# A first chunk's exponentials four heads at a time, finer gate steps, and a new order of the front

## The chip, the cores and the metric

The kernel runs on one core of a Trainium2 chip. The metric is device time in microseconds (us) of one execution. The kernel before takes 463.09 us, the median of three runs (462.23, 463.09 and 463.59).

The core has five engines, each with its own instruction queue that is worked off in order: TensorE (PE in the profile; its weight loads are shown as PEld), VectorE (DVE), ScalarE (ACT), GpSimd (POOL) and SyncE (SP). SP here issues nearly all transfers. Engines wait for each other by semaphores. TensorE writes its results into PSUM, a small memory of banks.

## The reference

An mLSTM cell over 4 batches, 8 heads, 768 time steps and 40 values per head, with a gate on its output, and behind it a two-layer network with an exact GELU. All is float32.

```python
for t in range(S):
    m_new = np.maximum(f_gate[:, :, t] + m, i_gate[:, :, t])
    f_stab = np.exp(f_gate[:, :, t] + m - m_new)
    i_stab = np.exp(i_gate[:, :, t] - m_new)
    m = m_new
    C = f_stab * C + i_stab * einsum('bhd,bhe->bhde', vt, kt)
    n = f_stab * n + i_stab * kt
    denom = np.maximum(np.abs(nq), 1.0)          # nq = n . q
    y[:, :, t] = sigmoid(o_gate[:, :, t]) * (C q) / denom
x = y as (3072 tokens, 320)
out = gelu(x @ w_in) @ w_out                     # w_in 320x2048, w_out 2048x320
```

The network's weights come as 64-bit floats, which the kernel reads as pairs of 32-bit words and turns into float32 itself.

## The kernel before

**Tiling.** The 768 steps are six chunks of 128. Within a chunk the cell is worked out like masked attention: scores of k and q, times a weight W = exp(a[key] - M[query]) where the key isn't behind the query, and then times v. What earlier chunks left is a state per batch and head. a, M and the decays come from the gates: bl is the running sum of f within a chunk, a = i - bl, M the running maximum of a, m0 the maximum carried from chunk to chunk. These gate tiles have 32 partitions (batch and head) and one row of 128 per chunk.

**Stages.** The program has a front and then five rounds. The front works out the gates, chunks 0 and 1 of the cell, and the network for chunk 0. Each later round works out one chunk of the cell beside the network for the chunk before. This case is about the front.

**The order.** In each engine's queue instructions stand in the order in which the program emits them. For the front that order is written out by hand in a string, `FRONT`. Each word is a step: a letter and, where needed, numbers (a batch, a chunk, a count). `play` runs them one after another, and each step puts its instructions into the queues of all engines that it uses. The letters:

- chunk 0 in lower case, chunk 1 in upper case, the number is the batch: `w`/`W` weights (the exponentials W, on ACT), `M` mask (POOL), `g`/`G` sigmoid of the output gate (ACT), `t`/`T` k and q transposed by TensorE and copied by ACT, `s`/`S` scores on TensorE and their product with W on VectorE, `c`/`C` the state carried on, `v`/`V` values on TensorE, `y`/`Y` finish (VectorE), `x`/`X` y transposed for the network, `R` split of x.
- `L` loads q and k, `O` loads v and the output gate, `B` loads M of chunk 1 for one batch (the number runs over batches of all chunks, so `L4` is batch 0 of chunk 1).
- `P` fetches a piece of the network's weights, `K` converts the next fetched piece on ACT (two activations), `J` ends that on VectorE (two instructions) and fetches the piece four further on. There are four buffers for fetched pieces, ten pieces of w_in and sixteen of w_out.
- `A` and `U` are the network's up steps for the first and the second half of chunk 0's tokens, four each, with a GELU on ACT behind each; two that follow each other directly are run as a pair. `F` is one of sixteen rows of the down product. `Z` splits a weight for the next round.
- `E` the gates of chunk 1, `N` those of chunks 2 to 5 with their decays, `D`, `Q`, `d`, `q` the decays transposed and spread, `r` and `p` send some of these out and back, `e` first blocks of chunk 2, `H` frees the gate tiles.
- `k` n: n matmuls whose result nobody reads. `I` n: n such matmuls ahead of the next step that writes a fresh bank. Both keep TensorE going.

**The exponentials of chunk 0.** In `Cell.weights`, for chunk 0, M has to be spread over all 128 partitions. It is cut into three bf16 parts (`M_parts`, 96 partitions), and for each head one matmul with a row of an identity (`row`) puts M of that head into a bank `pm` that holds four heads (L460). A matmul with `beyond`, 1e30 where the key is behind the query, adds the mask (L462). The exponential is then taken head by head, since a is added as the activation's bias, one value per partition: eight activations of 128x128 for each batch (L465). aT is a turned by TensorE (`gates_turned`, L252 and L253). Chunk 1 has M from a transfer (`load_M`) and uses the same L465.

**Lines that the steps touch.** Fillers L226 (`warm`) and L398 (`unread`); gates L270 to L277; M_parts L308 and L310; conversion L374, L375 (ACT), L385, L386 (VectorE), fetch L364; scores L537 and L540; state L575 to L595; values L655; finish L672 to L677; y transposed L695, its copy into first_x L700; up steps L804, L810 and GELU L814; down rows L1042; the next round's products L947.

Of the kernel before, what the change touches and what calls it, by code (L numbers as in the profile page):

```python
# [9 lines left out]
F32 = mybir.dt.float32  # L10
F32R = mybir.dt.float32r
BF16 = mybir.dt.bfloat16
U32 = mybir.dt.uint32
AF = mybir.ActivationFunctionType
OP = mybir.AluOpType

P = 128
# [7 lines left out]


FRONT = """
    I2 O0 g0 L0 P0 L1 E k1 t0 P1 P2 w0 k7 N k2 w1 O1 K L2 Q s0 O3 w2 q D
    k2 d P3 t1 w3 c0 L3 J v0 t2 K K y0 s1 I7 v1 I8 O2 J g1 L4 I5 c1 K I1
    I2 y1 s2 x0 t3 B4 O4 B5 g2 J x1 s3 v2 c2 L5 y2 H T0 x2 G0 v3 g3 c3 K y3  # L30
    M1 J L6 J A x3 M0 K W0 O7 K A O6 O5 J M2 W1 S0 C0 K J J T1 U U
    K L7 V0 K T2 r J J A G2 K G1 Y0 W2 S1 K M3 C1 A J S2 J K W3 K
    V1 C2 Y1 T3 J J U U S3 V2 K K J G3 J Y2 C3 X0 K V3 J K F J F
    K K B8 F J K F F J K F F F R0 X1 J J K F J F K X2 F J
    K F J Y3 K F R1 e J F Z B9 B10 F X3 R2 Z R3 F p"""
DOWN = """
    M0 F Z F L3 W0 M1 Z W1 S0 C0 F F h0 Q2 F K2 G1 D3 B3 Z V0 G2 M2 W2 M3 W3 V1 K3 Q3 F G0 S2 Z Y0 G3 C2 h2 F
    F Y1 X0 V2 V3 F N F j R0 Y2 Y3 X1 F F X2 R1 F R2 X3 R3 F"""
# [3 lines left out]
def kernel(  # L42
# [16 lines left out]
    nc = tc.nc  # L59

    B, H, S, D = q.shape
    L = P
    NCH = S // L
# [3 lines left out]
    BH = B * H  # L67
# [45 lines left out]
    W = {n: shared([P, H, L], F32, f"W{n}") for n in range(B - 1)}  # L113
# [7 lines left out]
    eye = gates.tile([P, P], BF16, name="eye")  # L121
    beyond = gates.tile([P, L], BF16, name="beyond")
# [15 lines left out]
    def swapped(c, b):  # L138

        return c > 1 and b % 2 == 1  # L140

    def load(n, first=0, end=4):

        if n >= NCH * B:
            return
        c, b = divmod(n, B)
        for src, dst in ((q, qb), (k, kb), (v, vb), (o_gate, None))[first:end]:
            if dst and swapped(c, b):
                x, to = src[b, :, c * L:(c + 1) * L, :].rearrange("h p d -> p h d"), dst[turn_of(n)][:, :, 0:D]
# [24 lines left out]
    def turn_of(n):  # L174

        return n % NLD if n < 2 * B else (n - 2 * B) % NQ
# [31 lines left out]

    keep = gates.tile([BH, NCH, L], F32, name="keep")
    bl = gates.tile([BH, NCH, L], F32, name="bl")  # L210
    a = gates.tile([BH, NCH, L], F32, name="a")
    M = gates.tile([BH, NCH, L], F32, name="M")
    ew = gates.tile([BH, NCH - 1, L], F32, name="ew")
    gg = gates.tile([BH, NCH - 1, L], F32, name="gg")
    m0 = gates.tile([BH, NCH], F32, name="m0")
    M_left = gg[:, 0:2]
    M_parts = gates.tile([3 * BH, L], BF16, name="M_parts")
    row = gates.tile([3 * BH, BH], BF16, name="row")
    for j in range(3):
        m = slice(BH * j, BH * (j + 1))  # L220
        nc.scalar.copy(out=row[m], in_=ident[m, m])

    def warm(n):
        cold = ps_h.tile([P, P], F32, name="cold", tag="h")
# [21 lines left out]
    def gates_turned(*parts):  # L246

        for src, dst in parts:
            n = dst.shape[1]
            pg = ps_tr.tile([P, n, BH], F32, name="pg", tag="tr")  # L250
            for c in range(n):
                nc.tensor.transpose(pg[:, c, :], src[:, c, :], ident[0:BH, 0:BH])  # L252
            nc.vector.tensor_copy(out=dst, in_=pg)  # L253
# [12 lines left out]

    def gates_of(c0, c1):

        flat = lambda t: t[:, c0:c1].rearrange("p c l -> p (c l)")
        nc.vector.tensor_tensor_scan(out=flat(bl), data0=flat(keep), data1=flat(f_sb), initial=0.0,  # L270
                                     op0=OP.mult, op1=OP.add)
        nc.vector.tensor_tensor(out=a[:, c0:c1], in0=i_sb[:, c0:c1], in1=bl[:, c0:c1], op=OP.subtract)
        for c in range(c0, c1):
            nc.vector.tensor_tensor_scan(out=M[:, c], data0=a[:, c], data1=a[:, c], initial=m0[:, c:c + 1],
                                         op0=OP.max, op1=OP.max)
            if c + 1 < NCH:
                nc.vector.tensor_tensor(out=m0[:, c + 1:c + 2], in0=bl[:, c, L - 1:L], in1=M[:, c, L - 1:L],  # L277
                                        op=OP.add)

    def decays_of(e0, e1, g0, g1):  # L280

        e, g = slice(e0, e1), slice(g0, g1)
        nc.vector.tensor_tensor(out=ew[:, e], in0=a[:, e], in1=M[:, e, L - 1:L].to_broadcast([BH, e1 - e0, L]),
                                op=OP.subtract)
        nc.vector.tensor_tensor(out=gg[:, g], in0=m0[:, g0 + 1:g1 + 1].unsqueeze(2).to_broadcast([BH, g1 - g0, L]),
                                in1=M[:, g0 + 1:g1 + 1], op=OP.subtract)
        nc.scalar.activation(out=ew[:, e], in_=ew[:, e], func=AF.Exp)
        nc.scalar.activation(out=gg[:, g], in_=gg[:, g], func=AF.Exp)
# [13 lines left out]


    gates_of(0, 1)
    left = M[:, 0]
    for j in range(3):
        part = M_parts[BH * j:BH * (j + 1)]
        nc.vector.tensor_copy(out=part, in_=left)  # L308
        if j < 2:
            nc.vector.tensor_tensor(out=M_left[:, j], in0=left, in1=part, op=OP.subtract)  # L310
            left = M_left[:, j]
    gates_turned((a[:, 0:1], aT[:, 0:1]))
    warm(6)

    def second_gates():
        gates_of(1, 2)
        nc.sync.dma_start(out=M_d[0], in_=M[:, 1])
        gates_turned((a[:, 1:2], aT[:, 1:2]))
        decays_of(0, 2, 0, 1)

    def later_gates():
        gates_of(2, NCH)
        nc.sync.dma_start(out=M_d[1:].rearrange("c p l -> p c l"), in_=M[:, 2:])
        gates_turned((a[:, 2:], aT[:, 2:]))
        decays_of(2, NCH - 1, 1, NCH - 1)


    w_src = {}
# [67 lines left out]
    def unread(bank):  # L396
        for _ in range(idle[0]):
            nc.tensor.matmul(bank, ident, ident, start=True, stop=True, skip_group_check=True)  # L398
        idle[0] = 0
# [25 lines left out]
    class Cell:  # L425
# [16 lines left out]
        def weights(self, b):  # L442

            n = self.c * B + b
            if self.c > 0:
                W[n] = M_n = Mb.pop(n)
            elif n not in W:
                W[n] = wts.tile([P, H, L], F32, name="W", tag="W")
            for h in range(H):
                r = b * H + h  # L450
                if self.c > 0:
                    src = M_n[:, h, :]
                else:


                    if h % 4 == 0:
                        pm = ps_mm.tile([P, 4, L], F32, name="pm", tag="b")
                        unread(pm[:, 0, :])
                        for j in range(4):
                            nc.tensor.matmul(pm[:, j, :], row[:, r + j:r + j + 1].to_broadcast([3 * BH, P]), M_parts,  # L460
                                             start=(j == 0), stop=False, skip_group_check=True)
                        nc.tensor.matmul(pm, eye, beyond.unsqueeze(1).to_broadcast([P, 4, L]), start=False, stop=True,  # L462
                                         skip_group_check=True)
                    src = pm[:, h % 4, :]
                nc.scalar.activation(out=W[n][:, h, :], in_=src, func=AF.Exp, scale=-1.0, bias=aT[:, self.c, r:r + 1])  # L465
            if n in (B, B + 1):
                load_M(n + 2)
# [666 lines left out]
    def first_blocks():  # L1134

        copy_chunk(2, range(1))
        for r in (32, 96):
# [2 lines left out]

    first_g = Hidden(False)
    n_pieces = range(len(pieces))
    steps = dict(P=fetch, L=lambda n: load(n, 0, 2), O=lambda n: load(n, 2, 4), B=load_M, E=second_gates, N=later_gates,
                 I=keep_clock, k=warm, D=lambda: decays_turned(0, 2, 0, 1), Q=lambda: decays_turned(2, NCH - 1, 1, NCH - 1),
                 d=lambda: decays_last(0, 1), q=lambda: decays_last(1, NCH - 1), r=halves_out, p=halves_back,
                 A=in_turn(first_up_steps(0)), U=in_turn(first_up_steps(1)), e=first_blocks, F=in_turn(first_down_steps(first_g)),
                 K=in_turn(lambda i=i: conv_one(i) for i in n_pieces), H=products_begin,
                 J=in_turn(lambda i=i: conv_two(i) for i in n_pieces), Z=split_weight)
    steps |= cell_steps(0, "mwgtscvyx") | cell_steps(1, "MWGTSCVYXR")
    play(FRONT, steps)  # L1150
    for c in range(1, NCH):
# [6 lines left out]
        steps = cell_steps(c + 1, "MWGTscVYXRLKQDCBSjh", g)  # L1158
# [36 lines left out]
```

## Time and profile before

| | |
|---|---|
| median of three runs | 463.09 us |
| the profiled execution | 462.86 us |
| its span, first to last instruction | 460.7 us |
| TensorE busy | 451.9 us, 98% |
| VectorE busy | 308.7 us, 67% |
| ACT busy | 243.7 us, 53% |
| GpSimd busy | 76.7 us, 17% |
| granted TensorE clock | 1.000 |
| TensorE's share of the chain that ended last | 95% |
| first up step, first down row, end of the front | 40.2, 91.7 and 127.3 us |

The profile is of one execution. Busy time is summed over the instructions of an engine, and idle time is put down to what ended it. The chain of work that ended last is followed back from the last instruction, at each step to what released it. A down row, an up step or a transposition in float32 shows as one or two records for each matmul of the program.

### The profile page before, as it was taken

How to read it: one execution, taken by the hardware profiler on the slowest of the kernel's cores; microseconds unless marked ns; L12 is line 12 of the kernel's file. 1: busy time of each engine (PE TensorE's matmuls, PEld its weight loads, DVE VectorE, ACT ScalarE, POOL GpSimd, SP SyncE). 2: the span in 40 equal slices, each digit the busy share in tenths (PEclk: the TensorE clock that was granted, in tenths of full speed). 3: DMA queues.
4: the chain of work that ended last, by engine and by line, in shares of the span. 5: the costliest groups of instructions: out<-in, count | busy, mean ns of one | idle time of the engine just before them, and what ended most of it. 6: DMA issues, size and time to landing. Idle time of an engine off the chain costs nothing.

```text
span 460.7 us, 13113 instructions
## 1 busy us (share of the span) xinstructions
PE 451.9 (98%) x5432; PEld 402.0 (87%) x5432; DVE 308.7 (67%) x661; ACT 243.7 (53%) x541; POOL 76.7 (17%) x117
## 2 busy tenths in 40 slices
PE   9999999999999998999999999999999999999996
PEld 8787888877788898998899998899998899988996
DVE  8677457573579987755578754578654577699950
ACT  7886999953244593113494113395113395257701
POOL 3001030000010432200542200542300422100000
PEclk9999999999999999999999999999999999999999
DMA  7999962295857655219945219853018950200001
GB/s 168 221 221 223 232 177 69 82 242 125 166 129 158 113 96 98 57 51 182 167 79 103 59 57 184 154 92 46 3 57 168 172 94 15 80 35 1 1 0 58
DMA packets 174875, 51.12 MB, mean 111 GB/s; under 512 B 154752, under 2 KB 168352, under 8 KB 174816
## 3 DMA queue, kind: packets, MB, share of 16 engines
q1 hardware_dynamic: 174496, 49.95, 51.0%
q8 instruction: 43, 0.70, 0.6%
q10 hardware_dynamic: 320, 0.33, 0.2%
q14 instruction: 16, 0.13, 0.1%
HBM read 45.47 MB, written 10.03 MB: 120 GB/s over the span
## 4 chain that ended last, share of the span: by engine, by line
PE 95%; DVE 2%; issue 1%; DMA 1%; ACT 1%; SPq 0%; DVEq 0%
PE po L1063 26%; PE pu L947 23%; PE po L1042 8%; PE pu L804 6%; PE pu L958 6%; PE po L917 6%; PE ph L655 4%; PE ps L553 3%; PE pu L810 2%; PE ps L537 2%; PE px L695 2%; PE pf L608 2%; PE pt L515 1%; PE cold L226 1%; PE pf L619 1%; PE pf L575 1%
## 5 line engine op out<-in xcount | busy, mean ns | idle before, releaser
L1063 PE MATMUL po<-w_out,g 128*128 128x160 f32 x512 | 74.4, 302 | 0.0
L962 ACT ACTIVATE g<-pu 128x512 f32<-128x512 f32 x64 | 32.2, 618 | 77.4 <-PE pu L958 77.4
L1063 PEld LDWEIGHTS po<-w_out,g 128*128 128x128 f32 x512 | 70.1, 190 | 1.9 <-ACT g L962 1.3
L947 PE MATMUL pu<-x_hi,w_in_hi 128*128 128x512 f32 x160 | 39.0, 387 | 0.0
L465 ACT ACTIVATE W<-W,aT 128x128 f32<-128x128 f32 x128 | 38.7, 387 | 0.1
L947 PE MATMUL pu<-x_lo,w_in_lo 128*128 128x512 f32 x160 | 37.8, 379 | 0.0
L1063 PE MATMUL po<-w_sums,sums 128*128 128x160 f32 x256 | 36.9, 302 | 0.0
L439 POOL TENSOR_SCALAR_AFFINE_SELECT W<-W 128x1024 f32<-128x1024 f32 (+2 forms) x20 | 24.1, 1209 | 75.8 <-DMA W<-M_d 66.8
L1063 PEld LDWEIGHTS po<-w_sums,sums 128*128 128x128 f32 x256 | 35.0, 190 | 0.4
L1042 PE MATMUL po<-w_out,g 128*128 128x320 f32 x128 | 35.2, 433 | 0.0
L947 PEld LDWEIGHTS pu<-x_hi,w_in_hi 128*128 128x128 f32 x160 | 29.5, 189 | 5.7 <-ACT g L962 1.3
L947 PEld LDWEIGHTS pu<-x_lo,w_in_lo 128*128 128x128 f32 x160 | 30.2, 189 | 4.3
L1042 PEld LDWEIGHTS po<-w_out,g 128*128 128x128 f32 x128 | 24.0, 190 | 9.6
L524 POOL TENSOR_TENSOR vw<-vb,ewT 128x328 f32<-128x328 f32 x12 | 8.7, 737 | 138.5 <-DMA vb<-in_v_dram 55.9
L947 PE MATMUL pu<-x_all,w_mid 128*128 128x512 f32 x80 | 30.3, 379 | 0.0
L947 PE MATMUL pu<-x_all,w_in_mid 128*128 128x512 f32 x80 | 30.3, 379 | 0.0
L559 DVE TENSOR_TENSOR W<-ps,W 128x256 f32<-128x256 f32 (+1 forms) x48 | 18.1, 416 | 17.0 <-PE ps L553 7.1
L804 PE MATMUL pu<-first_x,w_in 128*128 128x256 f32 x128 | 28.8, 381 | 0.0
L804 PEld LDWEIGHTS pu<-first_x,w_in 128*128 128x128 f32 x128 | 23.8, 190 | 3.1
L791 DVE TENSOR_TENSOR sums<-g 128x512 f32<-128x512 f32 x16 | 12.3, 770 | 19.6 <-ACT g L962 19.6
L763 DVE TENSOR_TENSOR w_in_mid<-w_in_hi,w_in_lo 128x512 fp32r<-128x512 f32 x20 | 13.7, 686 | 16.5 <-PE pu L947 16.5
L385 DVE SCALAR_TENSOR_TENSOR pow<-sig,pow 128x320 uint32<-128x320 uint32 (+1 forms) x26 | 14.6, 563 | 13.7 <-ACT pow L375 13.7
(195 smaller groups left out, 917.5 us busy)
## 6 DMA issues: line engine op xcount, KB each, us to landing
W<-M_d SPq DMA_DIRECT2D x16, 512.0 KB, 5.4
bits<-in_moe_w_in_dram SPq DMA_DIRECT2D x20, 256.0 KB, 4.5
bits<-in_moe_w_out_dram SPq DMA_DIRECT2D x16, 320.0 KB, 3.2
blocks<-kq_d SPq DMA_DIRECT2D x32, 128.0 KB, 3.6
ob<-in_o_gate_dram SPq DMA_DIRECT2D x24, 160.0 KB, 3.9
out_dram<-o_sb SPq DMA_DIRECT2D x36, 80.0 KB, 2.0
kq_d<-in_k_dram SPq DMA_DIRECT2D x32, 80.0 KB, 2.5
kq_d<-in_q_dram SPq DMA_DIRECT2D x32, 80.0 KB, 2.5
```

Of the source, the lines that this page charges most:

```text
L385: nc.vector.scalar_tensor_tensor(out=p, in0=s, scalar=3, in1=p, op0=OP.logical_shift_left, op1=OP.bitwise_or)
L439: nc.gpsimd.affine_select(out=x, in_=x, compare_op=OP.is_ge, fill=1.0e30, base=base, pattern=[[0, H], [1, x.shape[2]]], channel_multiplier=-1)
L465: nc.scalar.activation(out=W[n][:, h, :], in_=src, func=AF.Exp, scale=-1.0, bias=aT[:, self.c, r:r + 1])
L559: nc.vector.tensor_tensor(out=w[r, :, t], in0=ps[i][hip][r, :, t], in1=w[r, :, t], op=OP.mult)
L655: nc.tensor.matmul(ph[r, h, :], Pm[:, h, r], vb[turn_of(n)][:, h, :], start=True, stop=True)
L804: nc.tensor.matmul(banks[-1][e][:, i - i0, :], in_tile(i, x)[:, e, i % 2 * P:(i % 2 + 1) * P], first_x[:, x, t0:t1], start=(x == 0 and i = ...
L917: nc.tensor.matmul(in_pairs(po[t]), x[:, t * L:(t + 1) * L], in_turns(w), start=(f, k) == first, stop=(f, k) == last, skip_group_check=True)
L947: nc.tensor.matmul(in_pairs(pus[i][e]), w[k][:, e, i * P:(i + 1) * P], in_turns(x[:, k, :]), start=(n == 0 and k == 0), stop=False, skip_g ...
L958: nc.tensor.matmul(in_pairs(pu[e]), w[r, i // 2, i % 2 * P:(i % 2 + 1) * P], in_turns(x[r, NX, :]), start=False, stop=(n == 2), skip_group ...
L962: nc.scalar.activation(out=g.t[:, HF * e + i, :], in_=pu[e], func=AF.Gelu, scale=4097.0)
L1042: nc.tensor.matmul(po[b], g.t[:, f, b * L:(b + 1) * L], w_out[:, f, :], start=(f == 0), stop=(f == NF - 1))
L1063: nc.tensor.matmul(bank[k][:, t, :], lhs(j, t), rhs(j), start=(first and t == 0 and j == 0), stop=(t == 1 and j == HF - 1), skip_group_che ...
```

## The change

Three things are changed, all in the front.

1. **Chunk 0's exponentials.** a and M become two halves of one tile aM, and both are cut into three bf16 parts (`aM_parts`). `row` gets a second half with its sign turned. For each bank of four heads one matmul of 512 columns, with a's parts as the weights and the negated rows of four heads spread over 128 columns each, puts -a into the bank; four matmuls add M as before, and one the mask. One activation then takes the exponentials of four heads, 128x512, without a bias. aT of chunk 0 is no longer needed and its transposition goes.
2. **Later gates in parts.** `later_gates` (one step `N` for chunks 2 to 5) becomes `sums_of` for one chunk (`N2` to `N5`), `largest_of` for one chunk (`n2` to `n5`), the later decays (`l`), and the sending out and turning (`o`).
3. **The order.** All of `FRONT` is replaced. The old order has 28 fillers by `k` and `I`, the new one 19.

```diff
 FRONT = """
-    I2 O0 g0 L0 P0 L1 E k1 t0 P1 P2 w0 k7 N k2 w1 O1 K L2 Q s0 O3 w2 q D
-    k2 d P3 t1 w3 c0 L3 J v0 t2 K K y0 s1 I7 v1 I8 O2 J g1 L4 I5 c1 K I1
-    I2 y1 s2 x0 t3 B4 O4 B5 g2 J x1 s3 v2 c2 L5 y2 H T0 x2 G0 v3 g3 c3 K y3
-    M1 J L6 J A x3 M0 K W0 O7 K A O6 O5 J M2 W1 S0 C0 K J J T1 U U
-    K L7 V0 K T2 r J J A G2 K G1 Y0 W2 S1 K M3 C1 A J S2 J K W3 K
-    V1 C2 Y1 T3 J J U U S3 V2 K K J G3 J Y2 C3 X0 K V3 J K F J F
-    K K B8 F J K F F J K F F F R0 X1 J J K F J F K X2 F J
-    K F J Y3 K F R1 e J F Z B9 B10 F X3 R2 Z R3 F p"""
+    k2 L0 O0 t0 P0 N2 O1 N3 P1 L1 w0 k3 P2 N4 g0 E O3 n2 I5 w1 L2 N5 k7 n3 n4 n5 l Q t1 L3 K s0 K D J w2 q v0
+    w3 c0 y0 s1 g1 k2 K L4 O2 v1 t2 J P3 c1 y1 x0 g2 d s2 t3 O4 v2 c2 x1 B4 J y2 K s3 T0 g3 B5 x2 J K v3 A M1
+    y3 L5 K L6 M0 J x3 o J K W0 H K W1 A c3 O7 S0 C0 U J M2 O6 G0 O5 K K J J T1 r L7 e U A J T2 V0 K W2 S1 J K
+    S2 A G2 C1 G1 Y0 V1 U M3 J C2 K W3 V2 K T3 U J Z K Y1 J S3 K J K J J p K K C3 J G3 K F K F Y2 F K J F J V3
+    B8 X0 J B9 K K F R0 F X1 F K F X2 F F J J J F Y3 F R1 X3 B10 F R2 K F J F R3 J Z F"""
...
     for j in range(3):
         m = slice(BH * j, BH * (j + 1))
-        nc.scalar.copy(out=row[m], in_=ident[m, m])
+        nc.scalar.copy(out=row[m, 1], in_=ident[m, m])
+    nc.scalar.activation(out=row[:, 0], in_=row[:, 1], func=AF.Copy, scale=-1.0)
...
-    left = M[:, 0]
+    left = aM[:, :, 0]
...
-    gates_turned((a[:, 0:1], aT[:, 0:1]))
...
-    def later_gates():
-        gates_of(2, NCH)
+    def later_turned():
         nc.sync.dma_start(out=M_d[1:].rearrange("c p l -> p c l"), in_=M[:, 2:])
         gates_turned((a[:, 2:], aT[:, 2:]))
-        decays_of(2, NCH - 1, 1, NCH - 1)
...
-                        for j in range(4):
-                            nc.tensor.matmul(pm[:, j, :], row[:, r + j:r + j + 1].to_broadcast([3 * BH, P]), M_parts,
-                                             start=(j == 0), stop=False, skip_group_check=True)
+                    nc.tensor.matmul(pm, aM_parts[:, 0], row[:, 0, r:r + 4].unsqueeze(2).to_broadcast([3 * BH, 4, L]), start=True,
+                                     stop=False, skip_group_check=True)
+                    for j in range(4):
+                        nc.tensor.matmul(pm[:, j, :], row[:, 1, r + j:r + j + 1].to_broadcast([3 * BH, P]), aM_parts[:, 1],
+                                         start=False, stop=False, skip_group_check=True)
...
+                    nc.scalar.activation(out=W[n][:, h:h + 4, :], in_=pm, func=AF.Exp, scale=-1.0)
+                    continue
```

What follows from the new words for single steps: q and k of chunk 0's first batch are loaded ahead of v and the output gate; c3 and the turning of later gates (`o`) stand behind the first `A`; `U`, `A` are run as a pair, with `T2`, `V0`, `S1` and `S2` behind it; `r`, `e` and `p` stand much earlier; `V3` and `X0` stand between the `F`s; the last `J` and `Z` stand just ahead of the last `F`; the fetch of the fourth piece (`P3`) stands behind those of the fifth and sixth.

More of the change, by code (lines that the diff above doesn't have):

```diff
@@ L210 @@
     bl = gates.tile([BH, NCH, L], F32, name="bl")
-    a = gates.tile([BH, NCH, L], F32, name="a")
-    M = gates.tile([BH, NCH, L], F32, name="M")
+    aM = gates.tile([BH, 2, NCH, L], F32, name="aM")
+    a, M = aM[:, 0], aM[:, 1]
     ew = gates.tile([BH, NCH - 1, L], F32, name="ew")
@@ L215 @@
     m0 = gates.tile([BH, NCH], F32, name="m0")
-    M_left = gg[:, 0:2]
-    M_parts = gates.tile([3 * BH, L], BF16, name="M_parts")
-    row = gates.tile([3 * BH, BH], BF16, name="row")
+    aM_left = [gg[:, 0:2], gg[:, 2:4]]
+    aM_parts = gates.tile([3 * BH, 2, L], BF16, name="aM_parts")
+    row = gates.tile([3 * BH, 2, BH], BF16, name="row")
     for j in range(3):
         m = slice(BH * j, BH * (j + 1))
-        nc.scalar.copy(out=row[m], in_=ident[m, m])
+        nc.scalar.copy(out=row[m, 1], in_=ident[m, m])
+    nc.scalar.activation(out=row[:, 0], in_=row[:, 1], func=AF.Copy, scale=-1.0)
     def warm(n):
@@ L267, in gates_of, with sums_of @@
     def gates_of(c0, c1):
+        sums_of(c0, c1)
+        for c in range(c0, c1):
+            largest_of(c)
+    def sums_of(c0, c1):
         flat = lambda t: t[:, c0:c1].rearrange("p c l -> p (c l)")
@@ L272, in gates_of, with largest_of @@
         nc.vector.tensor_tensor(out=a[:, c0:c1], in0=i_sb[:, c0:c1], in1=bl[:, c0:c1], op=OP.subtract)
[L273 to L278, printed above, removed]
+    def largest_of(c):
+        nc.vector.tensor_tensor_scan(out=M[:, c], data0=a[:, c], data1=a[:, c], initial=m0[:, c:c + 1],
+                                     op0=OP.max, op1=OP.max)
+        if c + 1 < NCH:
+            nc.vector.tensor_tensor(out=m0[:, c + 1:c + 2], in0=bl[:, c, L - 1:L], in1=M[:, c, L - 1:L],
+                                    op=OP.add)
     def decays_of(e0, e1, g0, g1):
@@ L304 @@
     gates_of(0, 1)
-    left = M[:, 0]
+    left = aM[:, :, 0]
     for j in range(3):
-        part = M_parts[BH * j:BH * (j + 1)]
+        part = aM_parts[BH * j:BH * (j + 1)]
         nc.vector.tensor_copy(out=part, in_=left)
         if j < 2:
-            nc.vector.tensor_tensor(out=M_left[:, j], in0=left, in1=part, op=OP.subtract)
-            left = M_left[:, j]
-    gates_turned((a[:, 0:1], aT[:, 0:1]))
+            nc.vector.tensor_tensor(out=aM_left[j], in0=left, in1=part, op=OP.subtract)
+            left = aM_left[j]
     warm(6)
@@ L453, in weights @@
                 else:
-                    if h % 4 == 0:
-                        pm = ps_mm.tile([P, 4, L], F32, name="pm", tag="b")
-                        unread(pm[:, 0, :])
-                        for j in range(4):
-                            nc.tensor.matmul(pm[:, j, :], row[:, r + j:r + j + 1].to_broadcast([3 * BH, P]), M_parts,
-                                             start=(j == 0), stop=False, skip_group_check=True)
-                        nc.tensor.matmul(pm, eye, beyond.unsqueeze(1).to_broadcast([P, 4, L]), start=False, stop=True,
-                                         skip_group_check=True)
-                    src = pm[:, h % 4, :]
+                    if h % 4:
+                        continue
+                    pm = ps_mm.tile([P, 4, L], F32, name="pm", tag="b")
+                    unread(pm[:, 0, :])
+                    nc.tensor.matmul(pm, aM_parts[:, 0], row[:, 0, r:r + 4].unsqueeze(2).to_broadcast([3 * BH, 4, L]), start=True,
[3 more added lines that the diff above has]
+                                         start=False, stop=False, skip_group_check=True)
+                    nc.tensor.matmul(pm, eye, beyond.unsqueeze(1).to_broadcast([P, 4, L]), start=False, stop=True,
+                                     skip_group_check=True)
+                    nc.scalar.activation(out=W[n][:, h:h + 4, :], in_=pm, func=AF.Exp, scale=-1.0)
+                    continue
                 nc.scalar.activation(out=W[n][:, h, :], in_=src, func=AF.Exp, scale=-1.0, bias=aT[:, self.c, r:r + 1])
@@ L1142 @@
     n_pieces = range(len(pieces))
-    steps = dict(P=fetch, L=lambda n: load(n, 0, 2), O=lambda n: load(n, 2, 4), B=load_M, E=second_gates, N=later_gates,
+    steps = dict(P=fetch, L=lambda n: load(n, 0, 2), O=lambda n: load(n, 2, 4), B=load_M, E=second_gates, N=lambda c: sums_of(c, c + 1),
+                 n=largest_of, o=later_turned, l=lambda: decays_of(2, NCH - 1, 1, NCH - 1),
                  I=keep_clock, k=warm, D=lambda: decays_turned(0, 2, 0, 1), Q=lambda: decays_turned(2, NCH - 1, 1, NCH - 1),
```

## The prediction

> **What bounds the kernel now.** First the page's slices, then stretches cut where the chain of work that ended last changes character, then that chain, then groups and single rows.
>
> ```profile
> ACT  7886999953244593113494113395113395257701
> PEclk9999999999999999999999999999999999999999
> DMA  7999962295857655219945219853018950200001
> ```
>
> The change lies in the first eleven slices of 11.5 us. There DMA and ACT are nearly full and the granted clock is 9 everywhere. The same by stretches (columns: TensorE, its weight loads, DVE, ACT, POOL, each with its instructions; clock, DMA share, GB/s):
>
> ```profile
> 8.00:40.00 32.00, 29.92 (x419) 26.01 (x418) 23.67 (x60) 25.76 (x68) 0.36 (x1) 1.00 1.00 224
> 40.00:92.00 52.00, 52.00 (x680) 44.36 (x677) 31.83 (x69) 49.68 (x95) 6.33 (x6) 1.00 0.58 145
> 92.00:127.40 35.40, 35.40 (x139) 25.18 (x138) 19.44 (x49) 13.88 (x32) 0.74 (x1) 1.00 0.78 178
> ```
>
> From 40 us TensorE never idles and ACT rests 2.3 of 52 us; before it TensorE idles 2.1 of 32 us. The chain is TensorE's own from there:
>
> ```profile
> 40.20 3.65 PE pu L804 x16
> ...
> 91.69 17.42 PE po L1042 x64
> ...
> 125.17 2.16 PE po L1042 x8
> 127.33 10.36 PE pu L947 x48
> ```
>
> The first up step (A1) starts at 40.2, the first down row (F1) at 91.7, the front ends at 127.3. So the front is a TensorE budget: work, filler matmuls, idle. Rows that price the parts:
>
> ```profile
> L465 ACT ACTIVATE W<-pm,aT 128x128 f32<-128x128 f32 x32 | 8.6, 371 | 0.0
> ...
> L814 ACT ACTIVATE g<-pu 128x512 f32<-128x512 f32 x16 | 8.5, 599 | 1.9 <-PE pu L810 1.9
> ```
>
> ```profile
> 2.69 2.93 PE L226 MATMUL cold<-w_out 128*128 128x128 f32 x12
> ...
> 10.35 1.72 PE L226 MATMUL cold<-w_out 128*128 128x128 f32 x14
> ...
> 47.62 1.28 ACT L465 ACT_TABLE_LOAD   x1
> 48.92 2.45 ACT L465 ACTIVATE W<-W,aT 128x128 f32<-128x128 f32 x8
> ...
> 62.25 2.06 ACT L814 ACTIVATE g<-pu 128x512 f32<-128x512 f32 x4
> ```
>
> A filler matmul is two records of 123 ns (1.72/14); a table load is 1.28 us, and the next activation begins 0.02 us behind it.
>
> **The exponentials, on ACT.** 32 of them go (8.6 us) and 8 of 128x512 come. Four such gelus take 2.06 us, 0.52 each; alone one takes 0.60. So 4.2 to 4.8, I take 4.3: 4.3 saved. The new order has 16 table loads in the front, not 15 (+1.30); negating row is one small activation (0.2, the row copies). Net 2.8, all won before 40 us, where ACT rested 6.2 us anyway. Between the first and last gelu of the up steps the work grows: the extra table load 1.30, the sigmoid of ob0 (0.45) and batch 3's state copy (0.55), both earlier before: +2.3 us, where 2.3 us of rest were. The gain is spent where it isn't needed.
>
> The Trainium skill, "ScalarE: Activation LUTs", "What ACT_TABLE_LOAD costs", gives about 2.66 us for a switch, with a drain behind the load. The trace disagrees (1.28 + 0.02); by the rule the added switch would cost ACT 1.4 us more and the forecast would be up to that much later.
>
> **The spread gate, on TensorE.** Each of eight banks gets one more matmul of 512 columns in bf16. The chain gives the mask's, of the same size, 0.22, and 0.38 alone: 1.8 us (to 3.0). One transposition of a for chunk 0 goes, 0.1.
>
> **Fillers.** Behind the first transposition the old order has 27 (k7, k2, k2, and 2, 7, 5, 2 by keep_clock), which took 6.9 us by their start-to-start times; the new one 17 (k3, I5, k7, k2), 4.3 at the same rates. Minus 2.6. The start doesn't move: k now lands as the fourth load (o_gate, fourth before, was used at 5.6), but the start's fillers plus k2 end near 8.0, and the real work began at 8.0 behind fillers before.
>
> **The gates.** VectorE's three-part split is twice as wide: 1.34 us of five instructions becomes about 2.0 (0.40 for 32x256 against 0.28). Then sums_of four times at 0.75 (6.01 to 6.76) and the scan and addition of chunk 1 (0.69): done at 10.2. The next, the copy of aT, now waits for a transposition behind t0, w0 and k3 on TensorE: 8.0 + 1.0 + 1.3 + 0.7 = 11.1. From 11.3 stand 0.5 of chunk 1's decays, a sum of 0.75, four maxima (0.69 each, the last 0.5) and later decays of 1.1: to 16.3, where it was 14.3. ACT's last gate exponential (0.63) ends at 17.1. TensorE has done I5, w1 and k7 (1.3 + 1.3 + 1.7) by 15.6 and waits at Q: 0.7, 0.45, then 0.35 for the bank. Idle 1.5.
>
> **Chunk 0.** The first scores move from 15.4 to 18.5. From the first product at 19.65 VectorE is the long pole up to batch 3's product: four products 5.2, three finishes 5.1, J three times 4.1, three vw 1.4, copies 1.2: 17.0, so 36.7. TensorE's own 18.2 us from 18.5 end there too. Two waits for products behind a J or a finish, at v1 (0.5) and v2 (0.45): A1 near 38, two us earlier. But c3 (0.65) and four transpositions of a (0.43) now come behind A1, and V3 and X0 (1.2) behind F1.
>
> **SP and POOL.** k of chunk 1's batch 0 waits for c0's read of kb0, near 24.4, though SP is there near 18.6; v and o of batch 2 stand behind it. Landing 4.1 us (median; 6.5 at most) gives 29 to 31.5, v2 needs them near 32: hidden, and if c0 slips it slips v2 too. The fetch of w_in's eighth piece waits for the fifth's conversion (39.4), with two loads behind, due at 56: hidden by 10 us. r, e and p move forward; p's four issues leave 128.4 to 131.8, but the next stage's wait at 166 starts from TensorE's own L619, so nothing. e's clearing on POOL waits for T1; the w_out pieces behind its eight transfers are due from 97: hidden. The last J and Z now stand just ahead of the last F; VectorE has three F rows (6.5 us) for 3 us of R3, J and Z: nothing.
>
> **Up steps.** A2's second bank waits for batch 3's copy of first_x behind a gelu pair and a conversion: 0.3. S1 now follows U2, A3, T2 and V0 directly, and its banks are freed by T2's copies, which ACT does behind the four gelus. From A3's end: two gelus 1.08 and two copies 1.1 against T2 and V0, 1.75: 0.45 at least, 0.95 with ACT late; 0.7. S3: 0.2. Bounds from nothing to 3.
>
> **Sum.** +1.8 - 0.1 - 2.6 in work and fillers = -0.9. Idle 1.5 + 0.95 + 0.3 + 0.7 + 0.2 = 3.65 against 2.08 = +1.6. Together +0.7 us. The profiled execution took 462.86 (span 460.7), 0.23 under the median of 463.09; on the latter, 463.8. By the other route A1 stands at 38.0, then 51.5 - 1.2 + 1.1 of work and 1.2 of idle to F1, then 35.6 + 1.2: 127.4, no change; I keep the sum, which counts the fillers. Ends: no idle at all, -3.0 (460.1); idle doubled and the new matmuls at 0.38, +5.5 (468.6).
>
> **Rivals.**
> 1. Faster: ACT and VectorE lead TensorE everywhere, and most of the 3.65 vanishes. For it: ACT starts W0 near 9.8 instead of 10.2. Against it: VectorE's 17.0 us can't shrink and S1's 0.45 is in the order. Idle 1.2 gives 461.4. 0.23.
> 2. Slower: S1 behind the four gelus. ACT's work from the first gelu to T2's copies is about 25.1 us, TensorE's to V0's end 24.4, so it decides from there on: each us that ACT loses goes to TensorE. For it: 49.7 of 52 us busy and 2.3 more to do. At 2 us late 465.8. 0.29.
> 3. With fewer fillers TensorE slows as in its first us (244 ns a record against 123) somewhere in 15 to 37 us. For it: idle 1.5 us near Q. Against: idle of 0.96 us in 20 to 40 did nothing before. Four us at half speed lose 2: 465.8. 0.08.
>
> On the third, the Trainium skill, "TensorE: Matmul & The Clock Gate", "Part 1: The HAM clock gate", has the clock halved after an idle window of some 3.4 us, and Part 4 says that transpositions don't count as busy. The slow first records agree, though the clock row shows 9 there; no idle that I find is that long.
>
> **Numbers.** The forecast, near no change, has 0.40. 0.3% (1.4 us) is about what a measurement can tell; faster is rival 1, 0.23; slower 2 and 3, 0.37. Range 461.2 to 466.6, from rival 1 to just beyond 2 and 3; the forecast's own is 462.4 to 465.
>
> **What would show it.** ACT: eight W groups of 128x512 near 0.6 us. TensorE: A1 near 38, F1 near 90.8 with V3 and X0 behind it, the front's end near 128; idle at Q and S1. Wrong if A1 is later than 39 or idle in 40 to 92 exceeds 2 us, or if A1 comes by 37 and S1 doesn't wait.

## The result and the profile after

The changed kernel takes 464.62 us, the median of six executions (463.91 to 465.11); the kernel before took 462.66 beside it (462.11 to 463.59). The ratio is 1.0043, with a 95% interval of 1.003 to 1.0057: slower by 1.4 to 2.6 us. The forecast was +0.7 us, a change within 0.3%. The time lies in the range, and in the forecast's own 462.4 to 465; the change, 0.43%, is larger than the 0.3% of the likeliest case. The profiled execution is the slowest of the six (465.11); its span is 462.9 us, 2.2 more than before.

The slices, and the stretches, of the changed kernel (columns as before):

```profile
ACT  4877998965144593113394113394113396157701
PEclk9999999999999999999999999999999999999999
```

```profile
8.00:40.00 32.00, 30.47 (x396) 25.43 (x394) 25.22 (x71) 26.57 (x49) 0.00 (x0) 1.00 0.99 223
40.00:92.00 52.00, 51.87 (x617) 42.14 (x616) 24.65 (x52) 46.46 (x90) 6.22 (x6) 1.00 0.70 161
92.00:128.80 36.80, 36.80 (x206) 26.16 (x206) 26.35 (x63) 16.93 (x36) 2.85 (x3) 1.00 0.67 164
```

The clock is full. TensorE idles 1.5 us between 8 and 40 us (2.1 in the kernel before) and 0.13 between 40 and 92. By idle time alone nothing would seem to be lost. The chain of work that ended last shows it (start, length, what):

```profile
38.24 3.65 PE pu L811 x16
...
43.79 3.91 PE pu L811 x16
...
68.03 0.43 PE ps L544 x2
...
68.47 2.05 PE ps L544 x30
...
89.49 1.16 PE ps L544 x16
...
91.84 8.81 PE po L1049 x32
...
128.71 10.36 PE pu L954 x48
```

A1 starts at 38.24 (40.20 before), F1 at 91.84 (91.69), the front ends at 128.71 (127.33). The two microseconds won ahead of A1 are gone at F1, and 1.2 more go behind it. That is +1.38. The other 0.82 of the 2.2 arises **after** the front, where the change moved no instruction of TensorE. The same chain of the changed kernel in rounds 1 and 3:

```profile
177.07 0.44 PE pf L626 x16
177.51 1.37 issue
...
317.10 0.31 PE pf L626 x9
317.41 0.83 issue
```

And of the kernel before, where L619 is the same statement, in rounds 1 and 2:

```profile
175.68 0.24 PE pf L619 x5
175.92 1.11 issue
...
251.83 1.44 PE ph L655 x110
253.26 0.33 issue
```

"issue" is time in which TensorE waits for nothing that the profile shows: 2.20 us in the changed kernel, 1.44 before. The work from the start of the execution to each of these stops, first in the changed kernel and then in the kernel before (the first count in brackets is that of TensorE's matmul records):

```profile
0.00:177.52 177.52, 174.30 (x1997) 143.19 (x1998) 122.56 (x295) 123.11 (x247) 22.70 (x45) 1.00 0.72 159
0.00:317.42 317.42, 312.71 (x3902) 269.81 (x3902) 212.80 (x475) 182.55 (x389) 56.93 (x92) 1.00 0.64 136
```

```profile
0.00:175.95 175.95, 172.24 (x1997) 144.34 (x1997) 121.99 (x290) 125.40 (x269) 22.64 (x45) 1.00 0.72 160
0.00:253.27 253.27, 248.43 (x3138) 214.38 (x3139) 173.84 (x399) 156.20 (x345) 42.04 (x73) 1.00 0.66 144
```

In both kernels TensorE stops behind its 1997th record, and otherwise behind the 3138th or the 3902nd: at fixed counts, whatever instruction stands there. The theory that came from this (the block theory): TensorE gets its instructions in blocks, and where a run of short matmuls uses up a whole block faster than the next arrives, it stands still at the block's end. In the rounds such runs are the scores (64 records of L560), the products with the state (64 of L615 and 32 of L626), 160 together. The 1997th record is number 64 + 64 + 16 = 144 of such a run in the changed kernel, and number 133 before. The order and the fillers of the front only moved the run against the blocks.

The values that the experiments are read by, each from one profiled execution; the ratio is of medians, to the kernel before run beside it:

| kernel | A1 | front's end | rounds 1 to 4 | stops in them | ratio, 95% interval |
|---|---|---|---|---|---|
| before | 40.20 | 127.33 | 277.10 | 1.4 | 1 |
| changed | 38.24 | 128.71 | 277.92 | 2.2 | 1.0043 (1.003 to 1.0057) |
| e1: old exponentials | 41.9 | 132.39 | 278.60 | 2.8 | 1.0166 (1.0143 to 1.0189) |
| e2: exponentials alone | 40.72 | 127.84 | 276.50 | 0.8 | 1.0000 (0.9989 to 1.0012) |
| e3: changed, without k2 and k3 | 38.68 | 129.18 | 278.38 | 2.7 | 1.005 (1.0033 to 1.0067) |
| e4: changed, T2 ahead | 37.51 | 134.87 | 277.92 | 2.2 | 1.0236 (1.021 to 1.0262) |
| e5: changed, U3 beside U4 | 38.00 | 129.89 | 278.33 | 2.5 | 1.0072 (1.0058 to 1.0086) |
| p1: e2 and parts | 41.33 | 128.45 | 275.94 | 0.2 | 1.0026 (1.0017 to 1.0035) |
| f3: e2, 16 records fewer | 40.76 | 127.90 | 277.88 | 1.9 | 1.0048 (1.0031 to 1.0065) |
| f2: e2, 18 more | 40.74 | 127.86 | 276.06 | 0.5 | 0.9996 (0.9987 to 1.0005) |
| f1: changed, 32 more | 37.42 | 127.91 | 275.91 | 0.3 | 1.0008 (0.9999 to 1.0017) |
| h1: changed, 128 more | 38.90 | 129.37 | 278.25 | 2.4 | 1.0101 (1.008 to 1.0122) |
| g2: changed, start earlier | 37.5 | 128.13 | 276.20 | 0.8 | 0.9998 (0.9989 to 1.0006) |
| b1: before, 24 more | 39.9 | 128.26 | 276.05 | 0.5 | 1.0016 (1.0003 to 1.003) |

Rounds 1 to 4 are 275.4 to 276.0 plus the stops in every row.

### The profile page after: what moved, and what is told of

Same layout as the page of the kernel before. It is cut to its first block, busy times and chain, and to the rows that moved or that the text cites. A ratio compares the mean times of both kernels' runs of the same rounds, so it can differ in the third digit from the quotient of the medians.

```text
span 462.9 us, 13074 instructions
## 1 busy us (share of the span) xinstructions
PE 453.8 (98%) x5421; PEld 400.6 (87%) x5421; DVE 310.2 (67%) x666; ACT 241.4 (52%) x519; POOL 77.8 (17%) x117
## 4 chain that ended last, share of the span: by engine, by line
PE 93%; ACT 3%; DVE 2%; issue 1%; DMA 1%; SPq 0%; DVEq 0%
PE po L1070 26%; PE pu L954 23%; PE po L1049 7%; PE pu L965 6%; PE po L924 6%; PE pu L811 5%; PE ph L662 3%; PE ps L560 3%; PE ps L544 2%; PE pf L615 2%; PE px L702 2%; PE pu L817 2%; PE pt L522 1%; PE cold L224 1%; PE pf L626 1%
## 5 line engine op out<-in xcount | busy, mean ns | idle before, releaser
L954 PE MATMUL pu<-x_all,w_mid 128*128 128x512 f32 x80 | 30.3, 379 | 0.0
L954 PE MATMUL pu<-x_all,w_in_mid 128*128 128x512 f32 x80 | 30.3, 379 | 0.0
L811 PE MATMUL pu<-first_x,w_in 128*128 128x256 f32 x128 | 29.5, 384 | 0.0
L811 PEld LDWEIGHTS pu<-first_x,w_in 128*128 128x128 f32 x128 | 23.7, 190 | 3.6 <-ACT first_x L707 0.4
L691 ACT COPY y_rest<-ob 128x128 f32<-128x128 f32 x16 | 4.7, 294 | 32.2 <-DVE ob L684 20.2
```

Of the source, the lines that this page charges most:

```text
L811: nc.tensor.matmul(banks[-1][e][:, i - i0, :], in_tile(i, x)[:, e, i % 2 * P:(i % 2 + 1) * P], first_x[:, x, t0:t1], start=(x == 0 and i = ...
L954: nc.tensor.matmul(in_pairs(pus[i][e]), w[k][:, e, i * P:(i + 1) * P], in_turns(x[:, k, :]), start=(n == 0 and k == 0), stop=False, skip_g ...
```

## The experiments

**e1: the new order and parts, the old exponentials.**

```diff
-                    nc.tensor.matmul(pm, aM_parts[:, 0], ...)
...
-                    nc.scalar.activation(out=W[n][:, h:h + 4, :], in_=pm, func=AF.Exp, scale=-1.0)
+                    for j in range(4):
+                        nc.scalar.activation(out=W[n][:, h + j, :], in_=pm[:, j, :], func=AF.Exp, scale=-1.0,
+                                             bias=aT[:, 0, r + j:r + j + 1])
```

> The new order and the gates in parts stay; chunk 0's exponentials go back to one head at a time with a as the bias, without the spread matmul, and aT of chunk 0 is turned again. If the front is a budget of TensorE's work, 1.8 us of matmuls less and 0.1 more make it 1.7 us faster than the changed kernel (462.9). If the early chain through ACT decides, each pair of exponential groups takes 1.07 us longer (2.12 against 1.05) ahead of the later gates' exponentials, twice: Q comes 2 us later, the first product too, and the first up step (38.2 in the changed kernel) near 40; then 464.5 to 465.

Measured: 469.46 us (469.23 to 471.23). TensorE's waits, and its stretches with the granted clock third from the right:

```profile
PE pg L250 <- ACT ew L293: 3.3, 1, 3.3
```

```profile
16.00:20.00 4.00, 2.26 (x17) 1.78 (x19) 0.55 (x2) 2.89 (x9) 0.00 (x0) 0.92 1.28 182
20.00:24.00 4.00, 4.00 (x31) 3.35 (x29) 2.15 (x6) 3.57 (x9) 0.00 (x0) 0.50 1.07 230
24.00:28.00 4.00, 4.00 (x62) 3.26 (x63) 3.05 (x10) 2.48 (x11) 0.00 (x0) 0.73 0.05 11
```

ACT is late with the gates' exponentials, TensorE idles 3.3 us at Q, and then the clock is halved for some 6.8 us (worked out from the three stretches). Neither theory had that. In the new order the new exponentials are worth 1.2% of the time, of which some 0.6 us are larger stops in the rounds (2.8 against 2.2).

**e2: the new exponentials in the old order, gates in one piece.** (`FRONT` and `later_gates` as before.)

> The order and the gate steps of the kernel before; only the exponentials of four heads with the spread gate are new. By the budget of TensorE's work 1.7 us slower than before (464.4), less what ACT's 4.3 us take away of TensorE's 2.1 us of idle before 40 us: 463.0 to 464.4. If the exponentials bring what ACT saves, since ACT is nearly full to 92 us: 1 to 3 us faster than before, 460 to 462.

Measured: 462.25 us, no change, between the two expectations. Between 8 and 40 us ACT has 3.6 us less to do (22.14 of busy time against 25.76), and yet A1 comes 0.5 us later than before: the exponentials were not what TensorE waited for. In the profiled executions the level time is made of a front 0.5 us later and rounds 0.6 us shorter, with smaller stops. So most of what the change loses comes from the order, the parts or the stops.

**p1: e2 with the gates in parts at their old place.**

```diff
-    I2 O0 g0 L0 P0 L1 E k1 t0 P1 P2 w0 k7 N k2 w1 ...
+    I2 O0 g0 L0 P0 L1 E k1 t0 P1 P2 w0 k7 N2 N3 N4 N5 n2 n3 n4 n5 o l k2 w1 ...
```

> The old order and the new exponentials, with the gates of the later chunks in parts (N2 to N5, n2 to n5, o, l) one behind the other where they stood in one piece. VectorE has 0.66 us more for its four sums instead of one, ahead of the transposition that Q's waits follow. Theory (the order is what costs, not the parts): 462.2 to 462.9, with TensorE's idle time near 17 us up by at most 0.66. Rival (the parts cost the front's 0.9 us): 463.1 or more.

Measured: 463.4 us, on the rival's side, though the front of the profiled execution lost less than the 0.9 it named. VectorE's rows, e2 and then p1:

```profile
8.30 1.21 DVE L277 TENSOR_TENSOR_SCAN bl<-keep,f_sb 32x512 f32<-32x512 f32 x1
...
12.72 0.25 DVE L254 COPY aT<-pg 128x128 f32<-128x128 f32 x1
```

```profile
10.22 0.41 DVE L277 TENSOR_TENSOR_SCAN bl<-keep,f_sb 32x128 f32<-32x128 f32 x1
...
13.34 0.25 DVE L254 COPY aT<-pg 128x128 f32<-128x128 f32 x1
```

One sum of 512 columns takes 1.95 us with its scan, four of 128 take 0.65 each: 2.6. The copy of aT, A1 and the front's end are each 0.61 to 0.62 later. The delay runs straight through the front. The profiled execution is the fastest of the eleven (462.66) and no slower than before: what its front loses its rounds gain, with hardly a stop in them. So it shows 0.6 us in the front, and not where the 1.2 us lie by which the median is longer than before. With the parts in the new order but without the two stops (f1) the ratio is 1.0008: by the medians the new order takes some two thirds of it back.

**e3: the changed kernel without k2 at the head of the front and without k3 ahead of the transposition of a.**

> The changed kernel without the two fillers ahead of the first transposition and the three ahead of the transposition of chunk 1's a. If VectorE's chain (it waited 1.45 us there for that transposition, then is the long pole up to batch 3's product) sets the first up step, it comes 1.2 to 1.3 us earlier, at 37.0, and the whole is as much faster: 463.4. If TensorE's own work sets it, the wait at Q only grows and nothing is won: 464.6. If fewer fillers slow the clock, records of 123 ns grow to 240 ns and it is slower, 465 or more.

Measured: 463.94 us, ratio 1.005 (1.0033 to 1.0067); the profiled execution took 465.88. Its stretches:

```profile
12.00:16.00 4.00, 2.50 (x23) 2.16 (x22) 2.60 (x9) 3.43 (x7) 0.00 (x0) 0.98 1.02 254
16.00:20.00 4.00, 4.00 (x28) 3.48 (x29) 0.52 (x2) 2.72 (x5) 0.00 (x0) 0.59 1.29 190
```

Everything up to Q came earlier, the idle time there grew to 1.35 us in one piece, and behind it the clock fell. This is the third rival's mechanism. Five of its twelve executions took 465.6 to 466.2, with a granted clock of 0.995 or 0.996 over the whole run; the other seven took 463.0 to 464.3, all at 1.000. The median of those seven, 463.45, is 1.3 us above the kernel before, where the changed kernel is 2.0 above it: with the clock full, the kernel without these fillers is some 0.6 us faster than the changed kernel, though its stops, in the profiled execution, are larger (2.7 us against 2.2).

**e4: T2 ahead of the up steps U and A.** (`r L7 e U A J T2 V0` becomes `r L7 e T2 U A J V0`.)

> The changed kernel with T2 ahead of the pair of up steps instead of behind it, so that ACT copies its k and q ahead of the four gelus. If S1's wait for those copies costs what the trace shows (S1 and S2 took 2.5 us where two such steps take 1.8), it is 0.7 us faster: 463.9. If ACT is what is short from 40 to 92 us, the wait only moves to S3 behind T3, where the chain already runs through ACT, and nothing is won: 464.6.

Measured: 472.9 us, ratio 1.0236 (1.021 to 1.0262), which neither expectation had. One wait of TensorE, and the stretches around its end:

```profile
PE pt L522 <- ACT kT L525: 5.6, 1, 5.6
```

```profile
56.00:60.00 4.00, 0.65 (x6) 0.41 (x4) 0.00 (x0) 3.94 (x8) 2.94 (x3) 0.89 0.69 168
60.00:64.00 4.00, 1.79 (x9) 1.79 (x10) 2.58 (x4) 3.23 (x6) 1.13 (x2) 0.50 1.19 213
64.00:68.00 4.00, 4.00 (x16) 3.38 (x16) 1.54 (x3) 1.87 (x2) 0.00 (x0) 0.76 0.94 227
```

T2's banks are freed by T1's copies, and ACT reaches these only behind conversions and gelus, so the whole queue stood 5.6 us. From about 59.1 us, still within the wait, the clock was halved for some 6.8 us (worked out from the three stretches). Where the changed kernel has T2, its banks are long free and only S1 waits 0.7.

**e5: U3 beside U4 again.** (`V1 U M3 ... T3 U J` becomes `V1 M3 ... T3 U U J`.)

> The changed kernel with its last two products of the first pass's second half (U3, U4) one behind the other again, as before. Step theory: a pair shares its start and took 8.84 us against 4.71 and 4.70: 0.55 us less, 464.1 at the most 464.5. Rival: J and C2 then stand earlier than what ScalarE has ready, TensorE waits for it ahead of V2 or T3, and the time stays at 464.6 or grows.

Measured: 465.37 us, ratio 1.0072 (1.0058 to 1.0086): the rival. The profiled execution is the slowest of the five (466.76). In it the pair takes 8.84 us as expected, but two waits appear between 40 and 92 us, where the changed kernel has none of this size:

```profile
PE pf L582 <- DVE state L602: 0.9, 1, 0.9
PE ph L662 <- ACT pow L378: 0.8, 1, 0.8
```

So a single U where it stands costs 0.57 us and covers 1.7.

**f1, f3, f2: a few records more or fewer ahead of everything.** Only the very first fill changes. A filler is two records in the profile; a short one (L230) takes 0.04 us and a long one 0.49 at first, so records can be added at about the same time.

```diff
# f1, on the changed kernel: 32 more      # f3, on e2: 16 fewer      # f2, on e2: 18 more
-    fill(42)                             -    fill(42)              -    fill(42)
-    warm(6)                              -    warm(6)               -    warm(6)
+    fill(60)                             +    fill(33)              +    fill(52)
+    warm(4)                              +    warm(7)               +    warm(5)
```

> The changed kernel with 18 more short fillers (L230) and 2 fewer long ones (L224) in the very first fill, at about the same time: 32 records more on TensorE ahead of everything, nothing else. Theory (instruction blocks): in all six traces so far TensorE stands still, waiting for nothing that the profile shows, right after its 1997th, 3138th or 3902nd matmul record, and only where that record lies late in a run of some 160 short matmuls (scores L560, products with the state L615 and L626, or L662). In the changed kernel the 1997th and the 3902nd lie 144 and 137 records into such a run: 1.37 and 0.83 us. With 32 records ahead they lie 112 and 105 into it, the stalls at L626 go, and the time falls by up to 2.2 us, to about 462.4 to 463.0 (0.998 to 1.001 of before on this chip), with rounds 1 and 3 at about 69.9 and 69.4. Rival (what the rounds lose comes from the order: e, p, L7 and the blocks loaded elsewhere): the stalls stay, 464.0 to 464.8.

> The old order with the new exponentials alone, with 9 fewer short fillers and 1 more long one in the first fill: 16 records fewer. Block theory: the 1997th record, now 126 into the run of round 1, comes to lie 142 into it, and the 3902nd 133 into that of round 3: stalls of 1.2 to 1.4 and 0.7 to 1.0 us at L631 as in the changed kernel, the one in L667 goes; 463.2 to 463.9 (ratio 1.002 to 1.004), though the order is that of before. Rival (the order does it): no stalls at L631, 462.2.

> The old order with the new exponentials alone, with 10 more short fillers and 1 fewer long one in the first fill: 18 records more. Block theory: its one stall of 0.77 us in L667 at the 3138th record (109 records into 128 short matmuls) comes 18 records earlier in the run and goes: 461.4 to 461.8, faster than before by 0.1 to 0.2%. Rival: no change, 462.2.

f1: 462.82 us. Both stops at L626 are gone, rounds 1 to 4 are 2.0 us shorter. In the profiled execution the front ends 0.8 earlier as well, but only because it starts earlier (below). f3: 464.2 us, beside e2's 462.25, with e2's order and the same front to 0.06 us; the stops of the changed kernel appear in it, at the same counts (1997 and 3901):

```profile
176.25 0.43 PE pf L631 x14
176.68 1.19 issue
...
316.33 0.28 PE pf L631 x6
316.61 0.71 issue
```

The places are the block theory's forecast, and the sizes (1.19 and 0.71) lie at the lower end of what it named; the time is above its 463.2 to 463.9. With the order of before, the rounds lengthen all the same: this refutes that the order as such lengthens them. The medians differ by 2.0 us where rounds and front of the profiled executions differ by 1.4; the remaining 0.6 is not explained. f2: 462.12 us, no change, where the block theory had named 461.4 to 461.8; its stop at L667 shrank from 0.77 to 0.19, and another of 0.3 came one block earlier, behind the 3012th record.

**h1: the changed kernel with 128 records more.** (`fill(42)` and `warm(6)` become `fill(112)`.)

> The changed kernel with 70 short fillers more in its first fill in place of its 6 long ones: 128 records more ahead of everything, which is one block of the spacing of TensorE's stalls (1141 records for nine, 764 for six: 127). Block theory: with a whole block more, the stalls fall on the same instructions as in the changed kernel, not on none as with 32 more: at L625 (L626 of the changed kernel) in rounds 1 and 3, 1.2 to 1.5 and 0.7 to 1.0 us, right after the 2124th and the 4029th record or so; rounds 1 to 4 in 277.7 to 278.3, the time 464.0 to 465.0 (ratio 1.004 to 1.006). Rival (f1 was faster because it has more short fillers or a shorter first fill): stalls gone, 462.5 to 463.

The stops are back, on the same two instructions, one block later in the count:

```profile
177.73 0.44 PE pf L625 x16
178.16 1.50 issue
...
317.98 0.31 PE pf L625 x9
318.30 0.93 issue
```

```profile
0.00:178.17 178.17, 173.31 (x2125) 142.00 (x2126) 122.74 (x295) 123.39 (x247) 22.82 (x45) 1.00 0.71 159
```

So the effect has a period near 128 records, and the stops of f1 did not go because it has more short fillers: h1 has more still. The time, 466.77 us (466.04 profiled), is above the 464.0 to 465.0 that was expected. Part of it is a new stop of the same kind, inside the longer fill, which put off the first transposition to 8.57; the rest isn't seen in the profiled execution:

```profile
1.04 3.86 PE L230 MATMUL cold<-w_out 128*32 128x41 f32 x223 [1.04 <-DVE low_bits L234]
6.56 0.20 PE L230 MATMUL cold<-w_out 128*32 128x41 f32 x1 [1.65 <-issue]
```

**b1 and g2: versions meant to beat both.** b1 is the kernel before with `fill(55)` and `warm(5)`; g2 is f1 with k2 taken from the front's head and three fillers added behind k7.

> The kernel before with 13 more short fillers (L232) and 1 fewer long one (L226) in its first fill: 24 records more on TensorE, nothing of the change. Block theory: its stalls of 1.11 us (1997th record, 133 into the run of round 1) and 0.33 us (3138th, in L655) shrink to at most the 0.5 us that stayed with the same offset of the blocks in the old order with the new exponentials: rounds 1 to 4 in 276.1 instead of 277.1, 461.1 to 461.5, ratio 0.997 to 0.9985. Rival (the stalls belong to what the changed kernel does): no change, 462.2.

> The changed kernel with 34 records more in all: the first fill with 18 more short and 2 fewer long fillers, the two of k2 ahead of the first transposition moved behind k7 and one added, where TensorE waits for ScalarE's gates. Theory: the stalls at L626 stay away, the first transposition starts 0.25 to 0.5 us earlier, and what TensorE idles at the gates of the later chunks is filled, so that no run has the lower clock that the kernel without k2 and k3 showed around 15 to 20 us: 462.2 to 462.6, no run more than 2 us above the lowest. Rival (the gates, not the fillers, set when the first products start): as with the 32 records alone, 462.8; if the idle time just moves, a part of the runs 2 us higher.

b1: 463.04 us. The rounds did what was said (276.05), but the front ended 0.93 later though A1 came 0.3 earlier, with TensorE waiting 0.3 us for k and 0.6 for a weight in VectorE's hands; why the few fillers bring that was not pursued. Its ratio, 1.0016, is slower than before, where 0.997 to 0.9985 was expected. g2: 462.46 us, with no execution above 462.84. The first transposition then waits for its data, so the fillers could not give more:

```profile
7.14 0.63 PE L522 MATMUL pt<-ident,kb 128*128 128x128 f32 x4 [0.91 <-DMA kb<-in_k_dram]
```

So neither is faster than before.

## Why the prediction was near, and what it had wrong

- **The exponentials on ACT** went as said: eight W groups of 0.58 us, the gain where nothing waited for it. e2 confirms it with a ratio of 1.0000.

```profile
L470 ACT ACTIVATE W<-pm 128x512 f32<-128x512 f32 x8 | 4.5, 584 | 1.1 <-PE pm L468 1.0
```

- **The gates.** The copy of aT was put at 11.1 to 11.3 and began at 11.15; VectorE's end was put at 16.3 and was 15.9; idle at Q was put at 1.5 and was 0.95. p1 shows the parts' price in the front, 0.61.
- **A1** near 38: 38.24. **A2's wait** 0.3: L811 takes 3.91, not 3.65. **S1's wait** 0.7: S1 and S2 take 2.48 (0.43 + 2.05) instead of 1.78. **F1 to the front's end** 36.8: 36.87.
- **From A1 to F1, the first step that failed.** The second route had 51.5 - 1.2 + 1.1 of work and 1.2 of idle, 52.6, and 53.60 were measured. The waits are as forecast; what was mis-sized is the work. It was carried over from before, but U3 and U4 no longer follow each other (4.71 + 4.70 instead of 8.84: 0.57). The rest, 0.4, is in two single up steps, in which the records of the longer part take 3.65 us where the kernel before has 3.46. That this comes from the work of another kind ahead of them fits; no run isolates it. The sum that gave the forecast has the same gap: its terms of work are the matmuls and the fillers, and none is for the up steps.
- **The rounds, the second step that failed.** "So nothing" stood behind the steps that reach into the next stage, and the rounds were taken as unchanged. They lost 0.82 us in the profiled executions. The trace of before showed it: its chain had 1.11 us of "issue" at 175.92, and the change moves TensorE's count of records at that place by 11. f1, f3 and h1 show that this count decides. It was in none of the rivals, nor in the signs of being wrong, which look at A1 and at idle time alone: by those (A1 at 38.24, 0.13 us idle between 40 and 92) nothing was amiss.
- **The range.** That it holds the time is in part luck: less idle time than forecast at Q made up for some of the two terms that are in no sum and no rival.
- **The rivals.** The first (faster) fell: ACT and VectorE lead TensorE less than it needs. The second named S1 as the place, and there it was no worse than forecast; the change came out slower by other means. The third did not happen in the changed kernel, but in e1, e3 and e4, next door to it. On its rule: the Trainium skill, "TensorE: Matmul & The Clock Gate", "Part 1: The HAM clock gate", has the clock halved after an idle window of some 3.4 us. In two traces the clock fell later than that, in one sooner: in e1 it fell 5.1 us after the last filler (3.3 of them idle), in e4 3.5 us after the last up step (2.4 of them idle); in e3 it fell 2.2 us after the last filler (1.35 of them idle). Besides the idle time only transpositions stand between, in all three. It stayed halved for 3.4 us in e3 and for 6.8 in e1 and e4.

So of 2.2 us in the profiled executions 0.8 are stops in the rounds and 1.4 the front. From before to e2, p1 and the changed kernel the front grows by 0.5 (the exponentials in the old order), 0.6 (the parts) and 0.3 (the new order), from single profiled executions each. The 0.3 is less than the 0.8 by which the start varies (below), and the medians of p1 and f1 point the other way, so whether the new order itself costs or gains time in the front stays open. By the medians the changed kernel without its two stops (f1) is level with the kernel before with its own.

## What to carry to other kernels

An unrolled kernel can gain or lose half a percent, as this one did, by the number of instructions ahead of a dense run of short matmuls: look for "issue" in the chain of waits before and after, count the records up to it, and shift by a few cheap instructions before believing or blaming a reordering. Price a moved step with its neighbours: a pair that is split, or a bank that is freed behind another engine's queue, costs what the step itself does not show. Work taken from an engine that nothing waits for is worth nothing there, and may still be what makes another order possible.

## What the runs showed of the hardware that was not expected

**Stops at block ends.** They lie 1141 records apart for nine blocks (1997 to 3138) and 764 for six (3138 to 3902), 127 each, and last 0.2 to 1.65 us. Others lie on the same grid: g2's behind the 1870th record (127 ahead of the 1997th), f2's behind the 3012th (126 ahead of the 3138th), and the one in h1's fill behind the 223rd (15 times 126.8 ahead of its 2125th). They come where the block ends late in a dense run: in that of 160, number 133 cost 1.11 us, 137 0.83, 144 1.37, 154 1.44; at 112 in f1 there was none. The number does not set the size alone: at 144, e4 took 1.22 us, h1 1.50 and e5 1.58, and in the run of 128 (L655, L667) number 109 or 110 cost 0.33 and 0.77. The page has a queue for instructions (packets, MB, share), and TensorE's records:

```profile
PE 453.8 (98%) x5421; PEld 400.6 (87%) x5421; DVE 310.2 (67%) x666; ACT 241.4 (52%) x519; POOL 77.8 (17%) x117
...
q8 instruction: 42, 0.69, 0.6%
```

42 packets of 16.4 KB (0.69 MB / 42) for 10842 records make 258 records, or 129 matmuls with their weight loads, a packet: close to the 127 and 128 found (the kernel before: 43 packets, 126 matmuls). That this queue is what TensorE waits for is argued from these counts, not shown by a wait. The Trainium skill, "Runtime: NRT & Kernel Launch", "Instruction fetch mechanics", has instructions arrive in blocks of 16 KiB, 256 instructions, and the cost of a block's end "mostly hidden". The size agrees; if the stops are these block ends, their cost is not hidden in these runs of short matmuls.

**The start varies.** With the same first fill TensorE's records pass from 244 to 123 ns each at about 4.5 us in e4 and near 7 in the changed kernel's profile, though the clock row shows 1.00 throughout. The first transposition thus moved between 7.15 and 7.91 us, and f1's front, started at 7.10, took the same 120.8 us from there to its end as the changed kernel's; A1 comes 30.3 us behind the first transposition in e4, e5, f1 and the changed kernel alike. A single profile's front can be off by 0.8 us for that reason alone.
